# A scan followed by a mixture of adapters: a second output bank, transposes over a free bank, a split residual matmul and other groups

## The chip, the cores and the metric

One core of a Trainium2 chip. The metric is the time of one execution in microseconds (us), taken on the device; shorter is better. The profile gives, for one execution, the span from the first to the last instruction; in the runs here the time is about 1.8 us above the span of the same run (213.81 against 212.0 us).

Engine names as in the profile: PE is TensorE (matmuls), PEld its weight loads, DVE is VectorE, ACT is ScalarE, POOL is GpSimd, SP is SyncE, which issues the loads and stores.

## The reference

```python
def _attn_ref(a, b):                 # a, b: (8, 6400, 128) fp32
    for t in range(S):
        h = a[:, t] * h + b[:, t]    # a scan along the sequence
        out[:, t] = h

def _moe_ref(x, w_gate, A, B):       # x: (51200, 128), 8 experts of rank 16, best 2 of 8
    logits = x @ w_gate
    topk = best two of logits;  w = softmax of those two
    delta = sum over the two of  w * (x @ A[e]) @ B[e]
    return x + delta
```

So 52.4 MB are read and 26.2 MB written, and each row goes through the scan, a gating of 8 logits, a product with 8 x 16 gated columns, and the addition of the row itself (the residual).

## The kernel before

The 51200 rows are 100 units of 512. For each unit w the kernel adds operations to a plan with an estimated cost, a priority ("key") and the operations they wait for; the plan then fixes the order of each engine before the launch. The operations of a unit, with the names used below:

- A, B (TensorE): four fp32 transposes each, of a into the bank pA and of b into pB (two banks).
- aev (ACT): copy of pA; scan (VectorE): 512 steps from that copy and pB into xT (fp16).
- L (TensorE): logits into pL. Per group of units, gating: copy of pL (ACT), first maximum (VectorE), three steps on GpSimd, second maximum (VectorE), four steps on GpSimd, sigmoid (ACT).
- Z (TensorE): x times A of all experts into pZ (two banks); mul (VectorE): gated product zw.
- T (TensorE): transposes of zw into pT; tev (ACT): copy of pT.
- R (TensorE): expert matmul and residual matmul into pO; oev (ACT): copy of pO; then the store.

The matmul outputs lie in PSUM, in eight buffers of one bank each: pA, pB, pB, pL, pZ, pZ, pT, pO.

```python
    NZ, NO = 2, 1                               # banks of pZ and of pO
    groups = cut((), 4, (2, 1, 1))              # gating groups: 24 x 4, then 2, 1, 1
    ...
        pL = sb(nc.psum_tensor("pL", [128, 512], F32))
        pT = sb(nc.psum_tensor("pT", [128, 1024], F16))
        pO = [sb(nc.psum_tensor(f"pO{i}", [128, UT], F32)) for i in range(NO)]
    ...
            add(f"Z{w}", "pe", w + 5, 230.0, emit, [f"scan{w}", f"mul{w - NZ}", "cst"])
    ...     # mul{w} waits for Z{w}, the sigmoid of its group, T{w - 2}
            add(f"T{w}", "pe", w + 6, 225.0, emit, [f"mul{w}", f"tev{w - 1}", "idh"])
    ...
        def delta(w):
            def emit(h):
                for i in range(Q):
                    c = o[:, i * 128 : (i + 1) * 128]
                    h.matmul(c, zwT[w % 2][:, i * 128 : (i + 1) * 128], Bcat_h, start=True, stop=False)
                    last = h.matmul(c, x_block(w, i), ident_h[:, :], start=False, stop=True)
                return last
            add(f"R{w}", "pe", w + 6.5, 455.0, emit, [f"tev{w}", f"oev{w - NO}"])
    ...     # oev{w} on ACT waits for R{w}
```

Of the kernel before, what the change touches and what calls it, by code (L numbers as in the profile page):

```python
# [12 lines left out]
PRINT = False  # L13


class _Op:


    def __init__(self, name, eng, key, busy, lat, emit, deps, dma):
        self.name = name  # L20
        self.eng = eng
        self.key = key
        self.busy = busy
        self.lat = lat
        self.emit = emit
        self.deps = deps
        self.dma = dma
        self.signal = False
        self.done = None


class _Plan:
# [7 lines left out]
    def add(self, name, eng, key, busy, lat, emit, deps=(), dma=None):  # L40
        self.ops[name] = _Op(name, eng, key, busy, lat, emit, list(deps), dma)

    def schedule(self, dma_rate):
# [8 lines left out]
        end = {}  # L52
        cand = {e: [] for e in self.sems}
        free = {e: 0.0 for e in self.sems}
        link = 0.0
        for op in ops.values():
            if not left[op.name]:
                cand[op.eng].append((0.0, op))
        todo = len(ops)
        while todo:  # L60
            best = None
            for e, c in cand.items():
                if c:
                    t = max(free[e], min(r for r, _ in c))
                    if best is None or t < best[0]:
                        best = (t, e)
            t, e = best
            pick = min((x for x in cand[e] if x[0] <= t), key=lambda x: (x[1].key, x[0]))
            cand[e].remove(pick)
            op = pick[1]  # L70
            self.order[e].append(op)
            free[e] = t + op.busy
            if op.dma:
                link = max(link, t + op.busy + 1500.0) + op.dma[2] / dma_rate
                end[op.name] = link + op.lat
            else:
                end[op.name] = t + op.busy + op.lat
            todo -= 1
            for u in users[op.name]:
                left[u.name] -= 1  # L80
                if not left[u.name]:
                    cand[u.eng].append((max(end[d.name] for d in u.deps), u))
# [30 lines left out]
def bass_associative_scan_2x2__then__mixture_of_adapters_kernel(  # L113
# [20 lines left out]
    NZ, NO = 2, 1  # L134
    NOUT = 16

# [18 lines left out]
    groups = cut((), 4, (2, 1, 1))  # L155
# [11 lines left out]
    with ExitStack() as stack:  # L167
# [34 lines left out]
        pL = sb(nc.psum_tensor("pL", [128, 512], F32))  # L202
        pZ = [sb(nc.psum_tensor(f"pZ{i}", [128, UT], F32)) for i in range(NZ)]
        pT = sb(nc.psum_tensor("pT", [128, 1024], F16))
# [8 lines left out]
        def add(name, eng, key, busy, emit, deps=(), dma=None):  # L213
            lat = {"pe": 190.0, "dve": 120.0, "act": 150.0, "pool": 100.0, "sp": 100.0}[eng]
            plan.add(name, eng, key, busy, lat, emit, deps, dma)
# [115 lines left out]
        def logits(w):  # L331
# [9 lines left out]
            add(f"L{w}", "pe", w + 1, 140.0, emit, [f"scan{w}", f"lev{k - 1}", "cst"])  # L341

        def gating(k):
# [3 lines left out]
            key = u0 + n + 0.5  # L347
            fixed = 60.0 + 75.0 * (4 - n)
# [4 lines left out]
            def bc(t):  # L353
# [8 lines left out]
                [f"L{w}" for w in range(u0, u0 + n)] + [f"p4_{k - 2}", f"p3_{k - 2}", f"p6_{k - 2}"],  # L362
            )
# [10 lines left out]
                "pool",  # L374
                key,
                410.0,
# [5 lines left out]
                "pool",  # L382
                key,
                650.0,
# [5 lines left out]
                "pool",  # L390
                key,
                460.0,
# [13 lines left out]
                "pool",  # L406
                key,
                410.0,
# [5 lines left out]
                "pool",  # L414
                key,
                650.0,
# [5 lines left out]
                "pool",  # L422
                key,
                460.0,
# [5 lines left out]
                "pool",  # L430
                key,
                460.0,
# [13 lines left out]
        def z_mm(w):  # L446
# [5 lines left out]
            add(f"Z{w}", "pe", w + 5, 230.0, emit, [f"scan{w}", f"mul{w - NZ}", "cst"])  # L452

        def z_mul(w):
# [3 lines left out]
            zview = pZ[w % NZ][:, :].rearrange("p (q e r) -> p q e r", q=Q, e=E, r=R)  # L458
            oview = zw[w % 2][:, :, :].rearrange("p q (e r) -> p q e r", e=E)
            add(  # L460
                f"mul{w}",
                "dve",
                w + 5.5,
                600.0,
                lambda h: h.tensor_tensor(out=oview, in0=zview, in1=gview, op=ALU.mult),  # L465
                [f"Z{w}", f"sig{k}", f"T{w - 2}"],
            )

        def zw_tr(w):
            def emit(h):  # L470
                for i in range(Q):
                    last = h.transpose(pT[:, i * 128 : (i + 1) * 128], zw[w % 2][:, i, :], ident_h[:, :])  # L472
                return last

            add(f"T{w}", "pe", w + 6, 225.0, emit, [f"mul{w}", f"tev{w - 1}", "idh"])

        def t_evac(w):
# [5 lines left out]
                lambda h: h.copy(zwT[w % 2][:, :], pT[:, 0:UT]),  # L483
                [f"T{w}", f"R{w - 2}"],
            )

        def delta(w):
            o = pO[w % NO]

            def emit(h):  # L490
                for i in range(Q):
                    c = o[:, i * 128 : (i + 1) * 128]
                    h.matmul(c, zwT[w % 2][:, i * 128 : (i + 1) * 128], Bcat_h, start=True, stop=False)  # L493
                    last = h.matmul(c, x_block(w, i), ident_h[:, :], start=False, stop=True)  # L494
                return last

            add(f"R{w}", "pe", w + 6.5, 455.0, emit, [f"tev{w}", f"oev{w - NO}"])

        def o_evac(w):
            add(  # L500
                f"oev{w}",
                "act",
                w + 6.5,
                480.0,
                lambda h: h.copy(outt[:, w % NOUT, :], pO[w % NO][:, :]),  # L505
                [f"R{w}", f"st{store_of.get(w - NOUT)}"],
# [39 lines left out]
        print("plan", plan.span) if PRINT else None  # L546
# [49 lines left out]
```

## Time and profile before

The median was 221.71 us (three executions). The profiled execution has a span of 221.2 us.

The table of windows gives, for a stretch, the busy time of PE, PEld, DVE, ACT and POOL (with instructions), then the granted TensorE clock, the DMA share and GB/s. The kernel before, steady stretch and drain (from the last scan to the end):

```profile
40.00:190.00 150.00, 150.00 (x2156) 148.85 (x2155) 145.57 (x197) 131.96 (x270) 66.85 (x134) 1.00 1.05 398
197.35:221.20 23.85, 12.55 (x169) 10.21 (x166) 7.98 (x16) 13.14 (x29) 7.89 (x25) 0.84 0.39 145
```

In the steady stretch TensorE counts as busy all the time, its weight loads 99%, VectorE 97%, and DMA moves 398 GB/s. In the 23.85 us of the drain no engine is busy for more than about 55% (ACT, 13.14 us).

VectorE in that drain (timeline of the kernel before: start, duration, instruction, count, and in brackets the idle time before it and what ended it):

```profile
197.35 1.27 DVE L313 TENSOR_TENSOR_SCAN xT<-a_st,xT,pB 128x512 f16<-128x512 f32 x1
198.54 0.67 DVE L465 TENSOR_TENSOR zw<-pZ,g 128x512 f16<-128x512 f32 x1
...
202.77 0.69 DVE L465 TENSOR_TENSOR zw<-pZ,g 128x512 f16<-128x512 f32 x1 [0.51 <-PE pT L472]
...
204.63 0.69 DVE L465 TENSOR_TENSOR zw<-pZ,g 128x512 f16<-128x512 f32 x1 [0.71 <-PE pT L472]
206.51 0.69 DVE L465 TENSOR_TENSOR zw<-pZ,g 128x512 f16<-128x512 f32 x1 [1.18 <-PE pT L472]
```

The products come one every 1.87 us, each held up by the transposes. The transposes stand on TensorE behind R, which waits for both copies on ACT. ACT in the same stretch:

```profile
206.28 0.59 ACT L505 COPY outt<-pO 128x512 f32<-128x512 f32 x1 [0.64 <-PE pO L494]
206.77 0.59 ACT L483 COPY zwT<-pT 128x512 f16<-128x512 f16 x1
207.24 0.24 ACT L442 ACTIVATE g<-um 128x32 f32<-128x32 f32 x1
208.15 0.59 ACT L505 COPY outt<-pO 128x512 f32<-128x512 f32 x1 [0.67 <-PE pO L494]
```

This is a ring over single buffers: copy of pO, R, T, product, Z, one after the other.

### The profile page before, as it was taken

The numbers are of one execution on the slowest core, as the hardware profiler recorded it, in microseconds if no ns is written. First come the engines' busy times: TensorE is split into PE (matmuls) and PEld (weight loads), VectorE is DVE, ScalarE is ACT, GpSimd is POOL, SyncE is SP. The second block draws the span as 40 slices with busy tenths as digits, with TensorE's granted clock in tenths as the row PEclk, the third lists the DMA queues.
The fourth block names the chain that finished last, engine by engine and source line by source line (L and its number), as shares of the span: only waits on it lengthen the run. The fifth ranks groups of instructions, "written<-read, shape, count | busy, mean of one in ns | idle before, by whom it ended". The sixth has DMA issues, their size and how long they took to land.

```text
span 221.2 us, 6969 instructions
## 1 busy us (share of the span) xinstructions
PE 204.4 (92%) x2800; PEld 195.6 (88%) x2800; DVE 191.5 (87%) x261; ACT 174.2 (79%) x356; POOL 90.5 (41%) x195
## 2 busy tenths in 40 slices
PE   3889999999999999999999999999999999987552
PEld 2767889999999999999999999999999999985441
DVE  0499999999999999999999999999999999994320
ACT  3245589888889888888888898888899888876653
POOL 1016425435353543534445253443535435357400
PEclk9999999999999999999999999999999999999985
DMA  7999999999999999999999999999999999843434
GB/s 183 379 387 387 385 385 388 385 402 402 398 402 398 398 400 399 399 399 397 399 397 398 402 398 402 397 397 402 398 398 401 395 400 400 320 180 134 156 131 153
DMA packets 42208, 79.23 MB, mean 358 GB/s; under 512 B 3648, under 2 KB 3776, under 8 KB 42176
## 3 DMA queue, kind: packets, MB, share of 16 engines
q1 hardware_dynamic: 40848, 78.65, 94.3%
q8 instruction: 22, 0.36, 0.7%
q10 hardware_dynamic: 1328, 0.14, 0.5%
q14 instruction: 10, 0.08, 0.1%
HBM read 52.56 MB, written 26.21 MB: 356 GB/s over the span
## 4 chain that ended last, share of the span: by engine, by line
PE 82%; DVE 7%; ACT 3%; DMA 2%; issue 2%; POOL 1%; SPq 1%; DVEq 0%; ACTq 0%; POOLq 0%
PE pA L282 19%; PE pB L282 18%; PE pZ L449 12%; PE pO L493 10%; PE pO L494 10%; PE pT L472 9%; DVE xT L313 5%; PE pL L338 5%; DMA b_in<-in_b_dram 2%; DVE zw L465 2%; ACT outt L505 2%; ACT zwT L483 1%; SPq L266 1%; POOL pn L417 0%; ACT a_st L296 0%
## 5 line engine op out<-in xcount | busy, mean ns | idle before, releaser
L313 DVE TENSOR_TENSOR_SCAN xT<-a_st,xT,pB 128x512 f16<-128x512 f32 x96 | 120.0, 1250 | 3.4 <-PE pB L282 1.6
L505 ACT COPY outt<-pO 128x512 f32<-128x512 f32 x100 | 58.9, 589 | 28.3 <-PE pO L494 27.5
L465 DVE TENSOR_TENSOR zw<-pZ,g 128x512 f16<-128x512 f32 x100 | 67.3, 674 | 10.9 <-PE pT L472 5.8
L296 ACT COPY a_st<-pA 128x512 f32<-128x512 f32 x100 | 59.3, 593 | 12.8 <-PE pA L282 8.3
L282 PE MATMUL pA<-ident_f,a_in 128*128 128x128 f32 x400 | 63.1, 281 | 3.8 <-DMA a_in<-in_a_dram 3.8
L282 PE MATMUL pB<-ident_f,b_in 128*128 128x128 f32 x400 | 61.2, 277 | 0.1
L493 PE MATMUL pO<-cst_h,zwT 128*128 128x128 f16 x400 | 56.2, 221 | 4.8 <-ACT zwT L483 4.8
L483 ACT COPY zwT<-pT 128x512 f16<-128x512 f16 x100 | 58.9, 589 | 0.4 <-PE pT L472 0.4
L494 PE MATMUL pO<-ident_h,xT 128*128 128x128 f16 x400 | 56.2, 221 | 0.0
L282 PEld LDWEIGHTS pA<-ident_f,a_in 128*128 128x128 f32 x400 | 43.0, 143 | 5.3 <-DMA a_in<-in_a_dram 4.2
L282 PEld LDWEIGHTS pB<-ident_f,b_in 128*128 128x128 f32 x400 | 46.9, 142 | 0.9 <-DMA b_in<-in_b_dram 0.9
L494 PEld LDWEIGHTS pO<-ident_h,xT 128*128 128x128 f16 x400 | 45.1, 114 | 1.0
L493 PEld LDWEIGHTS pO<-cst_h,zwT 128*128 128x128 f16 x400 | 39.2, 99 | 6.3 <-ACT zwT L483 6.1
L449 PE MATMUL pZ<-cst_h,xT 128*128 128x128 f16 x400 | 40.7, 225 | 3.6 <-DVE zw L465 3.5
L472 PE MATMUL pT<-ident_h,zw 128*128 128x128 f16 x400 | 39.0, 220 | 0.0
L449 PEld LDWEIGHTS pZ<-cst_h,xT 128*128 128x128 f16 x400 | 26.4, 117 | 5.0 <-DVE zw L465 4.5
L338 PE MATMUL pL<-cst_h,xT 128*128 128x8 f16 x400 | 27.4, 174 | 1.3 <-DVE xT L313 0.9
L472 PEld LDWEIGHTS pT<-ident_h,zw 128*128 128x128 f16 x400 | 26.7, 98 | 0.0
L338 PEld LDWEIGHTS pL<-cst_h,xT 128*128 128x128 f16 x400 | 23.5, 117 | 3.6 <-DVE xT L313 3.4
L377 POOL TENSOR_TENSOR d_0<-Lg,m_0 128x128 f32<-128x128 f32 (+2 forms) x14 | 5.4, 388 | 36.2 <-DVE m_0 L369 36.2
L409 POOL TENSOR_TENSOR d_0<-Lg,m_0 128x128 f32<-128x128 f32 (+2 forms) x14 | 5.5, 390 | 25.7 <-DVE m_0 L401 25.7
L409 POOL TENSOR_TENSOR d_1<-Lg,m_1 128x128 f32<-128x128 f32 (+1 forms) x13 | 5.2, 397 | 23.7 <-DVE m_1 L401 23.2
(29 smaller groups left out, 114.5 us busy)
## 6 DMA issues: line engine op xcount, KB each, us to landing
a_in<-in_a_dram SPq DMA_DIRECT2D x49, 512.0 KB, 11.2
b_in<-in_b_dram SPq DMA_DIRECT2D x49, 512.0 KB, 11.3
out_dram<-outt SPq DMA_DIRECT2D x49, 512.0 KB, 11.1
a_in<-in_a_dram SPq DMA_DIRECT2D x2, 256.0 KB, 3.6
b_in<-in_b_dram SPq DMA_DIRECT2D x2, 256.0 KB, 4.3
out_dram<-outt SPq DMA_DIRECT2D x2, 256.0 KB, 2.0
cst_f<-in_moe_A_dram ACTq DMA_DIRECT2D x1, 64.0 KB, 4.0
cst_f<-in_moe_B_dram ACTq DMA_DIRECT2D x1, 64.0 KB, 4.4
```

Source lines behind the costliest of these rows:

```text
L282: last = h.transpose(view[:, i, :], ring[:, w % RING, i * 128 : (i + 1) * 128], ident_f[:, :])
L296: lambda h: h.copy(a_st[w % 2][:, :], pA[:, :]),
L313: last = h.tensor_tensor_scan(out=xT[:, x0 + lo : x0 + hi], data0=a_st[w % 2][:, lo:hi], data1=pB[w % 2][:, lo:hi], initial=init, op0=ALU. ...
L338: last = h.matmul(pL[:, c : c + E], x_block(w, i), wg_h)
L409: lambda h: h.tensor_tensor(out=v(d2[s]), in0=v(Lg[s]), in1=bc(m2[s]), op=ALU.subtract),
L449: last = h.matmul(pZ[w % NZ][:, i * 128 : (i + 1) * 128], x_block(w, i), Acat_h)
L465: lambda h: h.tensor_tensor(out=oview, in0=zview, in1=gview, op=ALU.mult),
L472: last = h.transpose(pT[:, i * 128 : (i + 1) * 128], zw[w % 2][:, i, :], ident_h[:, :])
L483: lambda h: h.copy(zwT[w % 2][:, :], pT[:, 0:UT]),
L493: h.matmul(c, zwT[w % 2][:, i * 128 : (i + 1) * 128], Bcat_h, start=True, stop=False)
L494: last = h.matmul(c, x_block(w, i), ident_h[:, :], start=False, stop=True)
L505: lambda h: h.copy(outt[:, w % NOUT, :], pO[w % NO][:, :]),
```

## The change

The intent is a shorter drain and an earlier start of the products:

1. R is split: the residual matmul (R) no longer waits for the copy of zw, only the expert matmul (D) does. The flag start is set on the first of the four blocks only (start=i==0).
2. pO gets two banks. To make room, pL and pT share one bank (pTL); the plan gets "banks", and keeps two engines from being in one at a time.
3. In the last 10 units every second transposition goes into pA, which is free then, and every second output copy goes to VectorE.
4. The last group is one of four units, gated on VectorE with priority; the first groups are 1, 1, 2.
5. Other priorities (Z, T, R, D).

```diff
-    NZ, NO = 2, 1
+    NZ, NO = 2, 2
+    TAIL = 10
+    KZ, KT, KR, KD = 8, 8.2, 8.6, 8.0
-    groups = cut((), 4, (2, 1, 1))
+    groups = cut((1, 1, 2), 4, ())
-        pL = sb(nc.psum_tensor("pL", [128, 512], F32))
-        pT = sb(nc.psum_tensor("pT", [128, 1024], F16))
+        pTL = sb(nc.psum_tensor("pTL", [128, 512], F32))
+        pT = pTL[:, 0 : UT // 2].bitcast(F16)
+        pL = pTL[:, UT // 2 : UT // 2 + GB * E]
 ...  (gating)
-            key = u0 + n + 0.5
+            key = u0 + n + (0.5 if k < len(groups) - 1 else -6)
+            ge = "dve" if k == len(groups) - 1 else "pool"      # seven steps, were "pool"
 ...  (transposes of zw, their copy)
+        def spare(w):
+            return w >= NU - TAIL and w % 2 == 1
+        def t_dst(w):
+            return pA[:, 0 : UT // 2].bitcast(F16) if spare(w) else pT
-            add(f"T{w}", "pe", w + 6, 225.0, emit, [f"mul{w}", f"tev{w - 1}", "idh"])
+            add(f"T{w}", "pe", w + KT, 225.0, emit,
+                [f"mul{w}", "idh", f"tev{w - 2 if w > NU - TAIL else w - 1}"] + [f"aev{NU - 1}"] * spare(w),
+                bank=t_bank(w))
 ...  (residual and expert matmul)
-            add(f"R{w}", "pe", w + 6.5, 455.0, emit, [f"tev{w}", f"oev{w - NO}"])
+            add(f"R{w}", "pe", w + KR, 226.0, emit_x, [f"scan{w}", f"oev{w - NO}", "idh"])
+            add(f"D{w}", "pe", w + KD, 226.0, emit_d, [f"R{w}", f"tev{w}", "cst"])
 ...  (output copy)
+            oe = "dve" if w >= NU - TAIL and w % 2 == 0 else "act"
```

In the plan's scheduler (not shown) an operation with a bank starts only when the last operations of the other engines on that bank have ended, and then waits for them.

More of the change, by code (lines that the diff above doesn't have):

```diff
@@ L10, with __init__ @@
 AX = mybir.AxisListType
-PRINT = False
 class _Op:
-    def __init__(self, name, eng, key, busy, lat, emit, deps, dma):
+    def __init__(self, name, eng, key, busy, lat, emit, deps, dma, bank):
         self.name = name
@@ L27, in __init__ @@
         self.dma = dma
+        self.bank = bank
         self.signal = False
@@ L38, in __init__, with add @@
         self.order = {e: [] for e in sems}
-    def add(self, name, eng, key, busy, lat, emit, deps=(), dma=None):
-        self.ops[name] = _Op(name, eng, key, busy, lat, emit, list(deps), dma)
+    def add(self, name, eng, key, busy, lat, emit, deps=(), dma=None, bank=None):
+        self.ops[name] = _Op(name, eng, key, busy, lat, emit, list(deps), dma, bank)
     def schedule(self, dma_rate):
@@ L55, in schedule @@
         link = 0.0
+        bank = {}
         for op in ops.values():
@@ L62, in schedule @@
             for e, c in cand.items():
-                if c:
-                    t = max(free[e], min(r for r, _ in c))
-                    if best is None or t < best[0]:
-                        best = (t, e)
-            t, e = best
-            pick = min((x for x in cand[e] if x[0] <= t), key=lambda x: (x[1].key, x[0]))
+                for x in c:
+                    other = [end[o.name] for o in bank.get(x[1].bank, {}).values() if o.eng != e]
+                    t = max([free[e], x[0]] + other)
+                    if best is None or (t, x[1].key) < best[:2]:
+                        best = (t, x[1].key, e, x)
+            t, _, e, pick = best
             cand[e].remove(pick)
             op = pick[1]
+            if op.bank:
+                held = bank.setdefault(op.bank, {})
+                op.deps += [o for o in held.values() if o.eng != e]
+                held[e] = op
             self.order[e].append(op)
@@ L211, in bass_associative_scan_2x2__then__mixture_of_adapters_kernel, with add @@
         plan = _Plan(sems)
-        def add(name, eng, key, busy, emit, deps=(), dma=None):
+        def add(name, eng, key, busy, emit, deps=(), dma=None, bank=None):
             lat = {"pe": 190.0, "dve": 120.0, "act": 150.0, "pool": 100.0, "sp": 100.0}[eng]
-            plan.add(name, eng, key, busy, lat, emit, deps, dma)
+            plan.add(name, eng, key, busy, lat, emit, deps, dma, bank)
         def add_dma(name, eng, key, emit, slot, nbytes, deps=()):
@@ L339, in emit @@
                 return last
-            add(f"L{w}", "pe", w + 1, 140.0, emit, [f"scan{w}", f"lev{k - 1}", "cst"])
+            add(f"L{w}", "pe", w + 1, 140.0, emit, [f"scan{w}", f"lev{k - 1}", "cst"], bank="TL")
         def gating(k):
@@ L346, in gating, with cost @@
             s = k % 2
-            key = u0 + n + 0.5
-            fixed = 60.0 + 75.0 * (4 - n)
+            key = u0 + n + (0.5 if k < len(groups) - 1 else -6)
+            ge = "dve" if k == len(groups) - 1 else "pool"
+            def cost(t):
+                return 200.0 if ge == "dve" else t
             def v(t):
@@ L362, in gating @@
                 [f"L{w}" for w in range(u0, u0 + n)] + [f"p4_{k - 2}", f"p3_{k - 2}", f"p6_{k - 2}"],
+                bank="TL",
             )
@@ L373, in gating @@
                 f"p1_{k}",
-                "pool",
+                ge,
                 key,
-                410.0,
+                cost(410.0),
                 lambda h: h.tensor_tensor(out=v(d1[s]), in0=v(Lg[s]), in1=bc(m1[s]), op=ALU.subtract),
@@ L381, in gating @@
                 f"p2_{k}",
-                "pool",
+                ge,
                 key,
-                650.0,
+                cost(650.0),
                 lambda h: h.tensor_scalar(v(pn[s]), v(d1[s]), 0.0, -1.0e30, ALU.is_ge, ALU.mult),
@@ L389, in gating @@
                 f"p3_{k}",
-                "pool",
+                ge,
                 key,
-                460.0,
+                cost(460.0),
                 lambda h: h.tensor_tensor(out=v(L2[s]), in0=v(Lg[s]), in1=v(pn[s]), op=ALU.add),
@@ L405, in gating @@
                 f"p4_{k}",
-                "pool",
+                ge,
                 key,
-                410.0,
+                cost(410.0),
                 lambda h: h.tensor_tensor(out=v(d2[s]), in0=v(Lg[s]), in1=bc(m2[s]), op=ALU.subtract),
@@ L413, in gating @@
                 f"p5_{k}",
-                "pool",
+                ge,
                 key,
-                650.0,
+                cost(650.0),
                 lambda h: h.tensor_scalar(v(pn[s]), v(d2[s]), 0.0, -1.0e30, ALU.is_lt, ALU.mult),
@@ L421, in gating @@
                 f"p6_{k}",
-                "pool",
+                ge,
                 key,
-                460.0,
+                cost(460.0),
                 lambda h: h.tensor_tensor(out=v(d1[s]), in0=v(d1[s]), in1=v(d2[s]), op=ALU.add),
@@ L429, in gating @@
                 f"p7_{k}",
-                "pool",
+                ge,
                 key,
-                460.0,
+                cost(460.0),
                 lambda h: h.tensor_tensor(out=v(um[s]), in0=v(d1[s]), in1=v(pn[s]), op=ALU.add),
@@ L450, in emit @@
                 return last
-            add(f"Z{w}", "pe", w + 5, 230.0, emit, [f"scan{w}", f"mul{w - NZ}", "cst"])
+            add(f"Z{w}", "pe", w + KZ, 230.0, emit, [f"scan{w}", f"mul{w - NZ}", "cst"])
         def z_mul(w):
@@ L457, in z_mul, with t_bank @@
             gview = g[k % 3][:, o : o + Q, :].unsqueeze(3).broadcast_to([128, Q, E, R])
-            zview = pZ[w % NZ][:, :].rearrange("p (q e r) -> p q e r", q=Q, e=E, r=R)
             oview = zw[w % 2][:, :, :].rearrange("p q (e r) -> p q e r", e=E)
+            deps = [f"sig{k}", f"T{w - 2}"]
+            src = pZ[w % NZ]
+            eng, busy, deps = "dve", 600.0, deps + [f"Z{w}"]
+            zview = src[:, :].rearrange("p (q e r) -> p q e r", q=Q, e=E, r=R)
             add(
                 f"mul{w}",
-                "dve",
+                eng,
                 w + 5.5,
-                600.0,
+                busy,
                 lambda h: h.tensor_tensor(out=oview, in0=zview, in1=gview, op=ALU.mult),
-                [f"Z{w}", f"sig{k}", f"T{w - 2}"],
+                deps,
             )
+        def spare(w):
+            return w >= NU - TAIL and w % 2 == 1
+        def t_dst(w):
+            return pA[:, 0 : UT // 2].bitcast(F16) if spare(w) else pT
+        def t_bank(w):
+            return "A" if spare(w) else "TL"
         def zw_tr(w):
@@ L471, in emit @@
                 for i in range(Q):
-                    last = h.transpose(pT[:, i * 128 : (i + 1) * 128], zw[w % 2][:, i, :], ident_h[:, :])
+                    last = h.transpose(t_dst(w)[:, i * 128 : (i + 1) * 128], zw[w % 2][:, i, :], ident_h[:, :])
                 return last
-            add(f"T{w}", "pe", w + 6, 225.0, emit, [f"mul{w}", f"tev{w - 1}", "idh"])
+            add(
+                f"T{w}",
+                "pe",
+                w + KT,
+                225.0,
+                emit,
+                [f"mul{w}", "idh", f"tev{w - 2 if w > NU - TAIL else w - 1}"] + [f"aev{NU - 1}"] * spare(w),
+                bank=t_bank(w),
+            )
         def t_evac(w):
@@ L482, in t_evac, with emit_x, emit_d @@
                 480.0,
-                lambda h: h.copy(zwT[w % 2][:, :], pT[:, 0:UT]),
-                [f"T{w}", f"R{w - 2}"],
+                lambda h: h.copy(zwT[w % 2][:, :], t_dst(w)),
+                [f"T{w}", f"D{w - 2}"],
+                bank=t_bank(w),
             )
         def delta(w):
-            o = pO[w % NO]
-            def emit(h):
+            def emit_x(h):
                 for i in range(Q):
-                    c = o[:, i * 128 : (i + 1) * 128]
-                    h.matmul(c, zwT[w % 2][:, i * 128 : (i + 1) * 128], Bcat_h, start=True, stop=False)
-                    last = h.matmul(c, x_block(w, i), ident_h[:, :], start=False, stop=True)
-                return last
-            add(f"R{w}", "pe", w + 6.5, 455.0, emit, [f"tev{w}", f"oev{w - NO}"])
+                    last = h.matmul(
+                        pO[w % NO][:, i * 128 : (i + 1) * 128],
+                        x_block(w, i),
+                        ident_h[:, :],
+                        start=i == 0,
+                        stop=False,
+                        skip_group_check=True,
+                    )
+                return last
+            def emit_d(h):
+                for i in range(Q):
+                    last = h.matmul(
+                        pO[w % NO][:, i * 128 : (i + 1) * 128],
+                        zwT[w % 2][:, i * 128 : (i + 1) * 128],
+                        Bcat_h,
+                        start=False,
+                        stop=True,
+                        skip_group_check=True,
+                    )
+                return last
+            add(f"R{w}", "pe", w + KR, 226.0, emit_x, [f"scan{w}", f"oev{w - NO}", "idh"])
+            add(f"D{w}", "pe", w + KD, 226.0, emit_d, [f"R{w}", f"tev{w}", "cst"])
         def o_evac(w):
+            oe = "dve" if w >= NU - TAIL and w % 2 == 0 else "act"
             add(
                 f"oev{w}",
-                "act",
+                oe,
                 w + 6.5,
-                480.0,
-                lambda h: h.copy(outt[:, w % NOUT, :], pO[w % NO][:, :]),
-                [f"R{w}", f"st{store_of.get(w - NOUT)}"],
+                600.0 if oe == "dve" else 480.0,
+                lambda h: (h.tensor_copy if oe == "dve" else h.copy)(outt[:, w % NOUT, :], pO[w % NO][:, :]),
+                [f"D{w}", f"st{store_of.get(w - NOUT)}"],
             )
@@ L545, in bass_associative_scan_2x2__then__mixture_of_adapters_kernel @@
         plan.schedule(390.0)
-        print("plan", plan.span) if PRINT else None
         block = sb(nc.Block())
```

## The prediction

> **What bounds the kernel now.** Three stages.
> 1. Ramp to about 24 us: VectorE scans from 6.3 us (timeline).
> 2. Steady state, 24 to 197 us: the table of windows shows matmul and weight loads both at 99-100% from 40 to 190 us, VectorE at 97%, DMA at 398 GB/s. The timeline shows TensorE without a gap: a unit of 512 rows takes 7.80 us / 4 = 1.95 us (A transposes start at 185.89 and 193.69). The chain of waits is 82% TensorE. The Trainium skill (Perfetto Trace Analysis, head note) calls matmul busy time a bad measure and weight-load busy a good one; here both agree, and the 55 ns pitch of the fp16 matmuls confirms it.
> 3. Drain: the last scan starts at 197.35 us, and 23.9 us follow. Nothing is saturated: TensorE 6.8 of 10.7 us, ACT 7.1, VectorE 5.9. Nine gated products (zw) remain and start 1.87 us apart, in a ring of latencies that the chain shows: zw 0.70 -> Z matmul 0.41 -> residual+expert matmul 0.65, in program order -> transpose 0.24 -> zw. There is one pO bank and one transpose bank. The last gatings (2, 1, 1 units) add GpSimd steps of 0.24-0.65 us.
>
> **What the change does.** Matmul, transpose and copy counts stay. Residual matmuls no longer wait for the zw copy, only the expert half does. pO gets a second bank by merging logits and transposes into one; the plan then keeps engines apart on that bank (the skill, PSUM — Partial Sum Buffer, Terms, calls two engines in one bank an error; no run here shows that). For the last 10 units, transposes alternate with the free pA bank and half of the output copies go to VectorE. The last group is four units, gated on VectorE: seven operations which I estimate at 0.2 us each, from the 0.28 us reduction and the 0.67 us product (512 elements), against 0.41-0.65 us on GpSimd.
>
> **Steady state: no gain.** Same TensorE work, already back to back. The order listing shows the same lag: when scan 16 or scan 96 is issued, 8 and 88 products have gone (before: 8 and 87). One unit more is done before the last scan: +0.7 us. I walked a cycle of four units: no chain exceeds 7.8 us. Loads: the last one issues at 178 us, lands about 190 us, is used at 193.7 us; one store now goes ahead earlier, about 1.3 us; slack remains.
>
> **Ramp:** two residual blocks go in earlier, small groups add reductions: 0 to +0.4 us.
>
> **Drain:** I walked the new order with traced durations. From the start of the last scan: gating done and sigmoid at 8.2 us, interleaved with four products; last four products end at 11.3; last expert matmul 13.3; last copy 14.0; store 2.6 (as before: 218.6 to 221.2). That is 16.6 us, plus 0.3 us for the lower clock that this sparse stage got before (0.53). 17 us instead of 23.9.
>
> Sum: last scan at 198.2, end at 215.2 us of span; timed runs are 0.5 us above it: **215.5 us** (-2.8%), range 212.5 to 219. Chances: faster 0.76, same 0.21, slower 0.03.
>
> **Signs.** Right: 40-190 us still 100% matmul and near 399 GB/s; last scan at 197.5-199; zw spacing in the drain below 1.3 us apart from one gap of under 2 us at the last gating; drain about 17 us. Wrong: TensorE gaps behind the merged bank (logits or transposes waiting for ACT), or transposes of a waiting for DMA at the end.
>
> **What would make it wrong.** The fixed order stalling TensorE in the steady state (1% is 2 us); VectorE gating slower than 0.2 us a step; the clock dropping earlier; or a ramp that saves more than I see.

## More of the kernel before

Timeline of the kernel before, a product on VectorE:

```profile
186.88 0.67 DVE L465 TENSOR_TENSOR zw<-pZ,g 128x512 f16<-128x512 f32 x1
```

and TensorE around its end, from T to the next A:

```profile
187.22 0.39 PE L472 MATMUL pT<-ident_h,zw 128*128 128x128 f16 x4
187.44 0.27 PE L338 MATMUL pL<-cst_h,xT 128*128 128x8 f16 x4
187.60 0.41 PE L449 MATMUL pZ<-cst_h,xT 128*128 128x128 f16 x4
187.85 0.61 PE L282 MATMUL pA<-ident_f,a_in 128*128 128x128 f32 x4
```

Busy times of matmuls overlap (0.27 us from 187.44 runs past 187.60), so only the distances of the starts tell the pace. L to Z is 0.16 us here. Z starts 0.05 us after the product ends, at 187.55.

## The result

The changed kernel took 214.12 us (median of four, 213.81 to 214.45) against 222.56 us before: ratio 0.962, 95% interval 0.956 to 0.968. Ratios here are the mean time of one kernel's runs over that of the other's in the same rounds, so not quite the ratio of the medians. The output was correct in all executions, before and after, and in all experiments.

Windows of the changed kernel, steady stretch and drain from the last scan:

```profile
40.00:190.00 150.00, 149.89 (x2180) 148.50 (x2179) 147.21 (x198) 128.41 (x273) 68.19 (x137) 1.00 1.05 398
195.59:212.00 16.41, 10.90 (x146) 8.36 (x144) 11.33 (x24) 9.21 (x19) 1.56 (x3) 1.00 0.55 204
```

The drain went from 23.85 to 16.41 us, and VectorE is busy 69% of it instead of 33%. The last scan comes 1.76 us earlier too. VectorE in the drain of the changed kernel:

```profile
195.59 1.27 DVE L319 TENSOR_TENSOR_SCAN xT<-a_st,xT,pB 128x512 f16<-128x512 f32 x1
196.98 0.69 DVE L553 COPY outt<-pO 128x512 f32<-128x512 f32 x1
197.59 0.27 DVE L379 TENSOR_REDUCE m_0<-Lg 128x16 f32<-128x128 f32 x1
...
198.58 0.68 DVE L478 TENSOR_TENSOR zw<-pZ,g 128x512 f16<-128x512 f32 x1
199.18 0.22 DVE L395 TENSOR_SCALAR pn<-d_0 128x128 f32<-128x128 f32 x1
199.31 0.68 DVE L478 TENSOR_TENSOR zw<-pZ,g 128x512 f16<-128x512 f32 x1
...
202.92 0.29 DVE L443 TENSOR_TENSOR um<-d_0,pn 128x128 f32<-128x128 f32 x1
203.59 2.70 DVE L478 TENSOR_TENSOR zw<-pZ,g 128x512 f16<-128x512 f32 x4 [0.37 <-ACT g L452]
```

No product waits for a transposition any more. The gating steps stand between the products, and the last four products wait for the gating alone.

ACT in the changed drain, the copies of the last transposes and outputs:

```profile
206.18 0.58 ACT L513 COPY zwT<-pTL 128x512 f16<-128x512 f16 x1 [0.22 <-PE pTL L494]
206.66 0.59 ACT L553 COPY outt<-pO 128x512 f32<-128x512 f32 x1
207.14 0.60 ACT L513 COPY zwT<-pA 128x512 f16<-128x512 f16 x1
208.31 0.58 ACT L553 COPY outt<-pO 128x512 f32<-128x512 f32 x1 [0.56 <-PE pO L533]
```

And the steady stretch of the changed kernel. The same transition of TensorE as above:

```profile
160.84 0.39 PE L494 MATMUL pTL<-ident_h,zw 128*128 128x128 f16 x4
161.06 0.27 PE L344 MATMUL pTL<-cst_h,xT 128*128 128x8 f16 x4
161.19 0.39 PE L459 MATMUL pZ<-cst_h,xT 128*128 128x128 f16 x4
161.42 0.61 PE L288 MATMUL pA<-ident_f,a_in 128*128 128x128 f32 x4
```

L to Z is 0.13 us now, not 0.16, and Z to A is 0.23, not 0.25 (the means between 60 and 180 us are 0.129 against 0.158, and 0.228 against 0.250). So these two held pauses of TensorE, not work. VectorE in a later cycle of the same kernel:

```profile
187.88 2.69 DVE L319 TENSOR_TENSOR_SCAN xT<-a_st,xT,pB 128x512 f16<-128x512 f32 x2
190.49 1.26 DVE L478 TENSOR_TENSOR zw<-pZ,g 128x512 f16<-128x512 f32 x2
191.67 0.27 DVE L379 TENSOR_REDUCE m_1<-Lg 128x16 f32<-128x128 f32 x1
191.86 1.27 DVE L319 TENSOR_TENSOR_SCAN xT<-a_st,xT,pB 128x512 f16<-128x512 f32 x1
193.05 0.66 DVE L478 TENSOR_TENSOR zw<-pZ,g 128x512 f16<-128x512 f32 x1
193.63 1.27 DVE L319 TENSOR_TENSOR_SCAN xT<-a_st,xT,pB 128x512 f16<-128x512 f32 x1
194.82 0.26 DVE L411 TENSOR_REDUCE m_1<-L_1 128x16 f32<-128x128 f32 x1
195.00 0.68 DVE L478 TENSOR_TENSOR zw<-pZ,g 128x512 f16<-128x512 f32 x1
```

Two scans stand next to each other here, and then two products (x2 counts them). From the first scan's start to the first product's it is 2.61 us; from a scan's start to that of a product behind it, it is 1.19 us (191.86 to 193.05). The experiments come back to this.

### Where the 9.2 us of span went

I took the starts of the copies of pA from the timelines of both kernels. The copy of unit 4 starts at 12.63 us before and 12.32 us after, but over all runs below anywhere from 12.0 to 14.1 us, for a reason that has nothing to do with the change (last section). So I count from there; "pace" is the distance of the copies of units 28 and 92, divided by 64.

| stretch, us | before | after | gain |
|---|---|---|---|
| start to copy of unit 4 | 12.63 | 12.32 | 0.3 (jitter) |
| unit 4 to 28 | 45.05 | 43.97 | 1.1 |
| unit 28 to 92 (pace 1.952, 1.926) | 124.94 | 123.29 | 1.65 |
| unit 92 to 99 | 13.68 | 13.64 | 0.0 |
| copy of unit 99 to last scan | 1.05 | 2.37 | -1.3 |
| last scan to end (drain) | 23.85 | 16.41 | 7.4 |

The drain is the main gain. But 1.65 us came from a pace that I had called fixed, and 1.1 us from units 4 to 28 (12 to 57 us; at unit 10, about 22 us, the changed kernel is still 1.1 us behind, at unit 20 it leads by 0.3), and 1.3 us went back before the last scan, where the changed order has one product more and stands with its last scan behind it.

### The profile page after: what moved, and what is told of

The parts are those of the page before. It is cut to its first block, busy times and chain, and to the rows that moved or that the text cites. A ratio compares the mean times of both kernels' runs of the same rounds, so it can differ in the third digit from the quotient of the medians.

```text
span 212.0 us, 7066 instructions
## 1 busy us (share of the span) xinstructions
PE 201.3 (95%) x2800; PEld 192.9 (91%) x2800; DVE 195.6 (92%) x273; ACT 166.7 (79%) x351; POOL 86.9 (41%) x188
## 4 chain that ended last, share of the span: by engine, by line
PE 77%; DVE 16%; issue 2%; DMA 2%; ACT 1%; SPq 0%; DVEq 0%
PE pB L288 18%; PE pA L288 18%; DVE xT L319 11%; PE pO L521 9%; PE pO L533 9%; PE pZ L459 9%; PE pTL L494 8%; PE pTL L344 5%; DVE zw L478 3%; DMA a_in<-in_a_dram 2%; DVE outt L553 1%; ACT outt L553 1%; SPq L272 0%; PE pA L494 0%; DVE m_0 L379 0%
## 5 line engine op out<-in xcount | busy, mean ns | idle before, releaser
L513 ACT COPY zwT<-pTL 128x512 f16<-128x512 f16 x95 | 56.9, 598 | 2.9 <-PE pTL L494 2.7
L288 PEld LDWEIGHTS pB<-ident_f,b_in 128*128 128x128 f32 x400 | 43.0, 143 | 1.0 <-DMA b_in<-in_b_dram 0.4
L521 PE MATMUL pO<-ident_h,xT 128*128 128x128 f16 x400 | 38.9, 220 | 1.5 <-ACT outt L553 0.7
L533 PE MATMUL pO<-cst_h,zwT 128*128 128x128 f16 x400 | 38.6, 219 | 0.3
L494 PE MATMUL pTL<-ident_h,zw 128*128 128x128 f16 x380 | 36.8, 220 | 0.0
L521 PEld LDWEIGHTS pO<-ident_h,xT 128*128 128x128 f16 x400 | 31.5, 114 | 3.1 <-DVE outt L553 1.3
L533 PEld LDWEIGHTS pO<-cst_h,zwT 128*128 128x128 f16 x400 | 27.5, 97 | 2.1 <-PE pO L521 0.7
L344 PE MATMUL pTL<-cst_h,xT 128*128 128x8 f16 x400 | 27.3, 174 | 1.2 <-DVE xT L319 1.0
L344 PEld LDWEIGHTS pTL<-cst_h,xT 128*128 128x128 f16 x400 | 23.6, 116 | 3.2 <-DVE xT L319 2.7
L494 PEld LDWEIGHTS pTL<-ident_h,zw 128*128 128x128 f16 x380 | 25.0, 98 | 0.1
```

Of the source, the lines that this page charges most:

```text
L288: last = h.transpose(view[:, i, :], ring[:, w % RING, i * 128 : (i + 1) * 128], ident_f[:, :])
L344: last = h.matmul(pL[:, c : c + E], x_block(w, i), wg_h)
L494: last = h.transpose(t_dst(w)[:, i * 128 : (i + 1) * 128], zw[w % 2][:, i, :], ident_h[:, :])
L513: lambda h: h.copy(zwT[w % 2][:, :], t_dst(w)),
L521: last = h.matmul(pO[w % NO][:, i * 128 : (i + 1) * 128], x_block(w, i), ident_h[:, :], start=i == 0, stop=False, skip_group_check=True,)
L533: last = h.matmul(pO[w % NO][:, i * 128 : (i + 1) * 128], zwT[w % 2][:, i * 128 : (i + 1) * 128], Bcat_h, start=False, stop=True, skip_gro ...
```

## The experiments

Twelve kernels. As the plan orders all engines anew when an operation changes, a "single part" below means that part and the order that follows from it, unless I say that the order was the same. "Aligned end" is the span minus the start of the copy of unit 4, from one profile each; the last column is its difference to the changed kernel's. The changed kernel stands for comparison at 214.12 us. The intervals of the ratios are +-0.5 to 0.7%, so differences of under 2 us between kernels are not settled by them alone. For these I use the aligned end, which agrees within 0.15 us where only something without effect was changed (before and b_ring, changed and a_noself), and the traces.

| run | what | median us | ratio to before (95%) | pace | drain | aligned end | to the changed kernel |
|---|---|---|---|---|---|---|---|
| before | | 222.56 | 1 | 1.952 | 23.85 | 208.57 | +8.89 |
| changed | | 214.12 | 0.962 (0.956-0.968) | 1.926 | 16.41 | 199.68 | 0 |
| b_ring | before, a GpSimd step cut | 222.39 | 1.002 (0.996-1.007) | 1.952 | 23.76 | 208.43 | +8.75 |
| b_groups | before, first groups 1, 1, 2 | 221.90 | 1.001 (0.994-1.007) | 1.942 | 25.57 | 208.70 | +9.02 |
| b_dve | before, maxima cut | 221.06 | 0.993 (0.986-0.999) | 1.936 | 23.61 | 206.44 | +6.76 |
| a_tail0 | no rotation | 218.54 | 0.982 (0.977-0.986) | 1.927 | 19.89 | 203.17 | +3.49 |
| a_poolgate | last gating on GpSimd | 213.40 | 0.960 (0.955-0.966) | 1.926 | 15.65 | 198.93 | -0.75 |
| a_fused | no split | 212.85 | 0.956 (0.950-0.962) | 1.910 | 18.54 | 198.59 | -1.09 |
| a_onebank | one output bank | 220.92 | 0.992 (0.986-0.998) | 1.963 | 21.77 | 207.11 | +7.43 |
| a_groups4 | first groups of four | 212.83 | 0.955 (0.948-0.962) | 1.918 | 17.70 | 198.23 | -1.45 |
| a_noself | no wait of TensorE for itself | 214.18 | 0.961 (0.954-0.968) | 1.926 | 16.30 | 199.57 | -0.11 |
| a_last211 | last groups 2, 1, 1 | 216.16 | 0.972 (0.965-0.979) | 1.927 | 18.16 | 201.57 | +1.89 |
| s_best | candidate | 211.98 | 0.952 (0.945-0.959) | 1.918 | 17.05 | 197.62 | -2.06 |
| f_warm | candidate | 212.51 | 0.954 (0.948-0.960) | 1.910 | 18.02 | 198.07 | -1.61 |

Drains compare only where the order up to the last scan is the same (changed, a_tail0, a_poolgate, a_noself); else a longer drain can mean that the last scan came earlier, with more products left. The aligned end has no such catch.

### What carries the drain

**a_onebank**: one output bank again.

```diff
-    NZ, NO = 2, 2
+    NZ, NO = 2, 1
```

> The changed kernel with one output bank, split kept. Theory BANKS: residual of the next unit cannot start before the copy of the last one, so TensorE waits and the drain is 2 to 5 us longer; the steady pace may rise above 1.927. Rival SPLIT: under 1 us.

Measured: 220.92 us. Nearly the whole gain is gone: the drain is 21.77 us (5.4 more) and the pace 1.963 (0.036 a unit more, 2.3 us over units 28 to 92). BANKS holds; the drain's loss is just above its range. TensorE in that kernel's drain:

```profile
211.23 0.41 PE L521 MATMUL pO<-ident_h,xT 128*128 128x128 f16 x4 [0.56 <-DVE outt L553]
211.70 0.40 PE L533 MATMUL pO<-cst_h,zwT 128*128 128x128 f16 x4
212.77 0.61 PE L521 MATMUL pO<-ident_h,xT 128*128 128x128 f16 x4 [0.68 <-ACT outt L553]
```

Each residual waits for the copy of the unit before, although the copies go to two engines in turn. The split and the rotation are of little use without the bank.

**a_tail0**: TAIL = 0, so neither the spare transposition bank nor output copies on VectorE. The order is the same as in the changed kernel up to the last units.

> The changed kernel without the rotation in the last 10 units: one transpose bank, all output copies on ACT. Same order until the last scan. Theory TAIL: ACT then does both copies of each unit and transposes wait for the single bank, about 1.1 us a unit instead of 0.65, so the drain from the last scan grows from 16.4 to 18 to 19.5 us and the total by 1.5 to 3 us. Rival: split and second output bank alone shorten the drain; then under 0.7 us.

Measured: 218.54 us, 4.4 us longer by the medians, 3.5 us by the aligned end; the drain is 19.89 us. TAIL holds, with a loss above its range (1.5 to 3 us). The run takes away the spare bank and the copies on VectorE together, so their shares stay open. The products wait for the single transposition bank again, 1.64 us apart:

```profile
207.20 0.69 DVE L478 TENSOR_TENSOR zw<-pZ,g 128x512 f16<-128x512 f32 x1 [0.96 <-PE pTL L494]
208.84 0.69 DVE L478 TENSOR_TENSOR zw<-pZ,g 128x512 f16<-128x512 f32 x1 [0.94 <-PE pTL L494]
```

**a_last211**: `groups = cut((1, 1, 2), 4, (2, 1, 1))`.

> The changed kernel with last groups of 2, 1, 1 as before (the last single unit gated on VectorE). Theory LAST: three more gatings put 2 x 7 GpSimd steps of 0.24 to 0.44 us and three sigmoids in the drain, so it is 1 to 3 us longer than with one group of four. Rival: the last unit's gating is on 32 columns instead of 128 and ends sooner, the products before it hide it; within 0.7 us of the changed kernel.

Measured: 216.16 us, 2.0 us longer (1.9 aligned). LAST holds: on VectorE the last product starts at 208.52 us, behind three gatings in a row, where the changed kernel ends its last at 206.29.

**a_poolgate**: the last gating on GpSimd like all others; same order until the last gating.

```diff
-            ge = "dve" if k == len(groups) - 1 else "pool"
+            ge = "pool"
```

> The changed kernel with the last gating on GpSimd as all others. Theory INTENT (as the change and my prediction have it): VectorE gating is faster, so the last four products start later than 8.0 us after the last scan's start, and the total grows by 1 to 2 us. Rival INTERLEAVE: on VectorE the seven steps stand between products and output copies and take 5.6 us from first maximum to last sum, on GpSimd about 4.6 us with VectorE free; then the last products start 0.3 to 1 us earlier, and the total is 0 to 1 us shorter.

Measured: 213.40 us. The drain is 15.65 us, 0.76 us less than with VectorE. INTERLEAVE holds: the last products start 7.24 us after the last scan's start (203.39 against 196.15), before 8.00 (203.59 against 195.59).

```profile
202.78 0.69 DVE L553 COPY outt<-pO 128x512 f32<-128x512 f32 x1 [0.97 <-PE pO L533]
203.39 2.69 DVE L478 TENSOR_TENSOR zw<-pZ,g 128x512 f16<-128x512 f32 x4
```

A step takes 0.22 to 0.29 us on VectorE against 0.41 to 0.65 on GpSimd. But on VectorE it stands in one line with products and output copies: from first maximum to last sum 5.6 us (197.59 to 203.21), on GpSimd 4.8 us (198.15 to 202.92), with VectorE free for the products. The part of the change that looked cheapest costs 0.75 us.

**a_fused**: residual and expert matmul in one operation again, as before; two banks, rotation, groups as changed.

```diff
 ...  (one emit with both matmuls per block, as before, in place of two)
-            add(f"R{w}", "pe", w + KR, 226.0, emit_x, [f"scan{w}", f"oev{w - NO}", "idh"])
-            add(f"D{w}", "pe", w + KD, 226.0, emit_d, [f"R{w}", f"tev{w}", "cst"])
+            add(f"D{w}", "pe", w + KD, 452.0, emit, [f"tev{w}", f"oev{w - NO}", "cst"])
```

> The changed kernel with residual and expert matmuls together again as before (both wait for the zw copy), two output banks, merged bank, rotation and groups kept. Theory BANKS: the second bank and the rotation carry the drain, the split does little, since the four residual matmuls take only 0.22 us: the total changes by less than 0.8 us. Rival SPLIT: getting the residual out of the chain is what shortens the drain; then it is at least 1.5 us longer.

Measured: 212.85 us, 1.3 us shorter than with the split (1.1 aligned). SPLIT falls. BANKS was right in that the split does not help, but I had not expected it to cost something. Its pace is 1.910, the fastest of all. The next experiments say why.

### What sets the pace

**b_ring**: the kernel before, with one GpSimd step of 0.46 us cut to one element (the output was still within the reference's tolerance); order unchanged.

> The kernel before, order of all engines kept, but the sixth gating step on GpSimd (the sum of the two differences, 0.46 us) reduced to one element. Results are wrong on purpose. Theory RING: before, the steady pace of 1.952 us a unit is set by a ring second maximum -> four GpSimd steps -> sigmoid -> product, in which VectorE waits 0.23 us in every four units for the sigmoid; taking 0.46 us out removes that wait and the pace falls to 1.925 to 1.935, so that the last a copy starts 1.5 to 2.5 us earlier and the total is about 2 us (0.9%) shorter. Rival PITCH: the pace is TensorE's own, from the order of its groups (transposes right behind logits take 0.47 instead of 0.44 us); then the pace stays at 1.950 +- 0.003 although the sigmoid wait is gone, and the total changes by less than 0.5 us.

Measured: nothing moved, 222.39 us, pace 1.952. The sigmoid wait of 0.23 us stayed as well, so the experiment did not do what it was meant to, and it can't decide between its theories. A look at ACT in the kernel before shows why:

```profile
191.31 0.59 ACT L505 COPY outt<-pO 128x512 f32<-128x512 f32 x1 [0.30 <-PE pO L494]
191.80 0.59 ACT L483 COPY zwT<-pT 128x512 f16<-128x512 f16 x1
192.27 0.32 ACT L442 ACTIVATE g<-um 128x128 f32<-128x128 f32 x1
```

The last GpSimd step had ended at 191.81 (191.35 plus 0.46), and the sigmoid starts at 192.27, when its turn on ACT comes. An earlier GpSimd does not help it. That gave RING2: TensorE up to R, then two copies and the sigmoid on ACT, product, maximum, scan and product on VectorE, then Z on TensorE.

**b_dve**: the kernel before, same order, both maxima over one block instead of 16 (0.07 us each instead of 0.19; the numbers of the gating are wrong on purpose, and stayed within the tolerance).

```diff
-                lambda h: h.tensor_reduce(out=m1[s][:, 0:c], in_=v(Lg[s]), axis=AX.X, op=ALU.max),
+                lambda h: h.tensor_reduce(out=m1[s][:, 0:1], in_=Lg[s][:, 0:1, :], axis=AX.X, op=ALU.max),
```

(and likewise m2; both cleared once at the start)

> The kernel before, order of all engines kept, with both maximum reductions cut to one block (0.19 us of VectorE each becomes about 0.07), wrong on purpose. The first ring test did not loosen the sigmoid wait, because the sigmoid stands on ACT behind the copy of pO and the copy of pT, not behind GpSimd. Theory RING2: the pace before, 1.952 us a unit, is closed by a ring through three engines: Z matmul waits for a product, TensorE 3.7 us, two copies and sigmoid on ACT, product, first maximum, scan, product, Z matmul. TensorE's own groups need only 1.926. Shortening the maximum by 0.13 us then brings the pace to 1.925 to 1.938, Z behind logits from 0.25 to 0.23 us, and the last a copy (taken from the copy of unit 24 on) comes 1.0 to 2.0 us earlier. Rival PITCH: VectorE is not in it, TensorE's order of groups costs that much; the pace stays at 1.950 +- 0.003.

Measured: pace 1.9355, within RING2's range and far from PITCH's; the last a copy comes 1.15 us earlier, counted from unit 24. On TensorE the mean distance of Z to the next A behind logits fell from 0.249 to 0.238 us, and in half of the cases the pause is gone:

```profile
185.64 0.27 PE L343 MATMUL pL<-cst_h,xT 128*128 128x8 f16 x4
185.77 0.39 PE L454 MATMUL pZ<-cst_h,xT 128*128 128x128 f16 x4
186.00 0.61 PE L287 MATMUL pA<-ident_f,a_in 128*128 128x128 f32 x4
```

So the kernel before was not TensorE at its own pace: a saving of 0.12 us on VectorE, twice in four units, moved a TensorE that counted as 100% busy. VectorE alone did not set the pace either, since its wait for the sigmoid grew from 0.23 to 0.37 us. That the ring runs through ACT is read from the timeline (the sigmoid behind two copies, and these behind R); no run shortened ACT.

**a_noself**: the changed kernel, same order, but D does not wait on TensorE's own semaphore (the counter by which an operation learns that another has ended) for R before it on the same engine (the waits for other engines stay).

```diff
             for d in op.deps:
+                if d.eng == eng == "pe":
+                    continue
                 sem, value = d.done
```

> The changed kernel, same order, but the expert matmul no longer waits on TensorE's own semaphore for the residual matmul before it on the same engine. Theory SELF: this wait drains the pipeline where the two follow each other (0.27 instead of 0.22 us, once in four units), the pace falls from 1.926 to 1.915 +- 0.003 us a unit and the total by 0.5 to 1.2 us. Rival: the 0.05 us are the wait for the copy of zw on ACT; no change of pace.

Measured: the pause went, R to D is 0.22 us now where it was 0.27 (mean of 15 and 14 cases between 60 and 180 us), but the pace stayed at 1.926, and the time at 214.18 us. So the wait was TensorE's for itself, as SELF says, and yet it cost nothing: in the same stretch A behind R starts after 0.249 us instead of 0.225, and R behind B after 0.455 instead of 0.443, so the pause came back elsewhere. TensorE, 99% busy in its weight loads, does not set the pace of the changed kernel. VectorE does: the lines of the changed kernel above show two scans in a row taking 2.61 us from 187.88 to the product at 190.49. The scan before a product takes 1.19 us, so the first of the two takes about 1.41. Its order repeats every four units (from 187.88 to 195.59, 7.71 us; the list of waits between 40 and 190 us has none of VectorE, and the trace has no idle time of it there but some 0.13 us between two scans in a row, 2.8 us in all): two scans, two products, maximum, scan, product, scan, maximum, product. That is 1.93 us a unit, the measured pace. In the order scan, product, scan, product no scan follows a scan. The second scan of a pair starts 0.13 us after the end of the first (187.88 plus 1.28 and 0.13, so at 189.29). It needs the last element of the first, and by the plan it also waits on VectorE's own semaphore for it, as D did on TensorE's. Where a unit of two sequences is scanned in two halves inside one operation, without such a wait and without that need, the second half (256 columns) starts 0.65 us after the first, before the first has ended (it counts as 0.74 us). No run separates the wait from the need; a_noself took away the waits of TensorE only.

With that, a_fused falls into place: its VectorE order is scan, product, scan, product almost throughout, and its TensorE order has no L in front of fp32 transposes except once in four or more units. Adding the distances of its groups (0.443 + 0.436 + 0.447 + 0.223 + 0.129 + 0.228 for A, B, R with D, T, L, Z) gives 1.906 us, next to its pace of 1.910. By itself such a sum is close to the pace in any kernel whose TensorE has no other groups; what counts is that no distance holds a pause: L to Z (0.129) and Z to A (0.228) are as short as in the changed kernel, where TensorE had time to spare. So this kernel seems to run at TensorE's own pace, with VectorE, which waits 1.2 us in 150, close behind; no experiment on it tests that.

### The start

**b_groups**: the kernel before with `groups = cut((1, 1, 2), 4, (2, 1, 1))`.

> The kernel before with first groups of 1, 1 and 2 units, last groups of 2, 1, 1 kept. Theory GROUPS: the 1.3 us that the changed kernel leads by at unit 20 come from the small first groups (products start at 16.4 instead of 22.3 us), so this kernel leads the kernel before by 1.0 to 1.6 us at unit 20 and is about 1.3 us shorter if its new order keeps the steady pace. Rival SPLIT: the lead comes from residual matmuls that fill TensorE early; then the lead at unit 20 is under 0.4 us.

Measured, counted from unit 4: a lead of 0.5 us at unit 20, 1.5 at unit 24, and an aligned end 0.1 us later than before. (Counted so, the changed kernel leads by 0.3 us at unit 20 and by 1.0 at unit 24; the 1.3 us of the expectation was too much.) A lead of the scans is no gain by itself: the drain grew from 23.85 to 25.57 us, the products that had not been made came later. Neither theory saw that; the small groups alone save nothing.

**a_groups4**: the changed kernel with `groups = cut((), 4, ())`.

> The changed kernel with first groups of four (25 groups of 4, last one still four units). Theory GROUPS: counted from the copy of unit 4 (to leave the slow first transposes out, which differ from run to run by up to 1.4 us), the small first groups gave 0.8 to 1.1 us at unit 24; without them this kernel is that much behind at unit 24 and 0.5 to 1.3 us longer. Rival: the lead is given back, because the lag of products behind scans is the same from unit 16 on; total within 0.5 us or even shorter.

Measured: 212.83 us, 1.3 us shorter (1.45 aligned), so the rival holds and more. Without the small groups, VectorE's order has scans and products in turn, and the pace is 1.918. That is 0.5 of the 1.45 us, over units 28 to 92; another 0.5 lies between units 4 and 28 (43.45 against 43.97) and 0.4 behind unit 92. The small first groups had shifted the order of the whole run, and cost time all along it.

### Candidates

**s_best**: the changed kernel with groups of four, gating on GpSimd, no wait of TensorE for itself, and seven matmuls on the identity from 1.5 us.

```diff
+        def warm_up(h):
+            for i in range(7):
+                last = h.matmul(pZ[0][:, 0:128], ident_f[:, :], ident_f[:, :])
+            return last
+        add("warm_up", "pe", -9, 2000.0, warm_up, ["id"])
 ...  (and the edits of a_groups4, a_poolgate and a_noself)
```

> Candidate: the changed kernel with groups of four throughout, last gating on GpSimd, no wait of TensorE for itself, and seven idle matmuls on the identity at 1.5 us so that the slow first transposes (1.1 us for four instead of 0.6) are paid while TensorE waits for the first load. If the single effects add: 1.3 + 0.7 + 0.8 + 1 us off 214.1, so 210.3 us, 209 to 212. Rival: loads bind (they land at about 188 us in the changed kernel and b of unit 98 is transposed at 191); then transposes of the last units show waits for DMA and the total stays above 212.

Measured: 211.98 us, the lowest median (the single times of f_warm, median 212.51, overlap with its own): 1% under the changed kernel, ratio 0.952 to before. No transposition waits for DMA in the last 30 us, so the rival falls, but the sum was 210.3: the self-wait was worth nothing, and so was the start.

**f_warm**: a_fused with the same seven matmuls.

> Candidate: the kernel with residual and expert matmul together (212.85 us) with the seven idle matmuls at the start. Theory CLOCK: the copy of unit 4, which starts at 12.1 to 14.1 us in all runs so far, starts below 12 us, and the total is 0.5 to 2 us shorter than 212.85. Rival: idle matmuls end in time but TensorE is as slow after them; then the copy of unit 4 is not earlier.

Measured: 212.51 us, 0.3 us under a_fused. The copy of unit 4 starts at 12.03 (12.48 in s_best), not below 12. The clock part is right, the gain is not: behind the idle matmuls the first four transposes take 0.60 us instead of 1.12, but they start at 4.65 instead of 3.5 to 3.8 us, and then the first scan starts at 6.29 us, as without. On VectorE it stands behind the cast of the constants, whose load lands at about 6 us.

```profile
6.07 0.30 DVE L261 CAST cst_h<-cst_f 128x264 f16<-128x264 f32 x1 [4.34 <-DMA cst_f<-in_moe_B_dram]
6.29 1.21 DVE L326 TENSOR_TENSOR_SCAN xT<-a_st,pB 128x512 f16<-128x512 f32 x1
```

Not run, and so open: the fused matmul together with groups of four and the gating on GpSimd; the first scan ahead of the cast; the old priorities (part 5 of the change); one output bank without the split; the changed kernel without VectorE's waits for itself. The second output bank was run with the merged bank only; in the changed kernel's steady stretch the list of waits has no wait of TensorE for a copy on it.

## Why the prediction was right or wrong

The time was right: 215.5 us predicted, 214.12 measured, in the range, and faster by over 2% with a chance of 0.76. Its parts were less so.

- **The drain: right.** "17 us instead of 23.9": 16.41. The last copy came 13.3 us after the last scan's start (predicted 14.0), the store took 3.1 (2.6), and the clock did not fall (0.3 us set aside). a_onebank, a_tail0 and a_last211 show that bank, rotation and the single last group carry it. The sign "one gap of under 2 us" was off: the gap is 2.6 us.
- **"Steady state: no gain. Same TensorE work, already back to back": wrong**, 1.65 us over units 28 to 92. The step that failed was to read 100% matmul and 99% weight-load busy as TensorE without a pause. The Trainium skill (Perfetto Trace Analysis, Identifying the Most-Contended Engine) names MFU (the matmul work done as a share of the peak), which I did not work out, and weight-load busy as the measures for TensorE; in this trace the latter reads 99% before, while pauses of 0.02 to 0.03 us at Z were hidden in it, and 99% after, while VectorE set the pace. The distance of the starts shows what the busy time hides. "I walked a cycle of four units: no chain exceeds 7.8 us" was about the new order only; the ring that held the old one, 7.81 us around, I did not look for. b_dve shows that VectorE is in it.
- **"Ramp: 0 to +0.4 us": missed.** By the end of what I called the ramp (about 22 us, unit 10) the changed kernel's copies are 1.1 us later, counted from unit 4; at unit 28 they are 1.1 us earlier. But 1.3 us are given back before the last scan, and b_groups shows that such a lead need not be a gain.
- **"Last scan at 198.2"**: 195.59, the sum of both points and of a product more, which did not cost the 0.7 us I had added.
- **"Timed runs are 0.5 us above" the span: wrong.** I compared the median of three executions with the span of another one, which had run 1.2 us longer. The offset is 1.8 us. With it, my span of 215.2 (measured 212.0) would have given 217.0 us. So two errors, 3.2 us in the span and 1.3 in the offset, partly cancelled.
- **Gating on VectorE "at 0.2 us each"**: the steps were 0.22 to 0.29 us, and the sigmoid was done 8.0 us after the last scan's start (predicted 8.2). But I compared it with the engine's speed and not with the line it would stand in; a_poolgate shows it costs 0.75 us. That the split would be a part of the gain I took from the change's intent; a_fused shows the opposite.
- **The merged bank**: the feared waits did not come. I named the skill's rule of one engine per bank (PSUM — Partial Sum Buffer, Terms); the plan kept to it in all runs, so no run shows what breaking it does.

## What to carry to other kernels

Where several engines are each 90 to 100% busy, look at the distances of the starts, and cut a little from one engine without changing the order: what moves tells who sets the pace. In this drain latency counted and not speed: give each buffer of the ring a second one, spread the copies over two engines, and leave work off the engine that the rest of the drain needs, even if another engine is twice as slow. Undo each part of a bundled change by itself: here the bank, the rotation and the single last group carried the gain (7.4, 3.5 and 1.9 us when one of them is taken away; they overlap, since the whole gain is 8.9), and three other parts (the split, the last gating on VectorE, the small first groups) cost about 0.75 to 1.45 us each.

## What the Trainium skill lacked or had wrong

- Perfetto Trace Analysis, Identifying the Most-Contended Engine: MFU and weight-load busy as the measures for TensorE. Here weight-load busy is 99% in both kernels (148.85 and 148.50 of 150 us), and in neither TensorE alone set the pace (b_dve: 0.12 us off each maximum on VectorE took 0.017 us a unit off; a_noself: a pause less on TensorE changed nothing).
- TensorE: Matmul & The Clock Gate, Part 4, says that the full clock "doesn't engage" for transposes. Here the first fp32 transposes run at half pace (1.12 us for four) and go over to 0.61 to 0.69 us: 3.4 to 4.8 us after the first one in the changed kernel (between 6.83 and 8.24 us, when TensorE had run 16 transposes and 12 fp16 matmuls), 7.8 to 9.5 us after it in b_ring (between 11.55 and 13.26 us). The start jitter goes with it: the copy of unit 4 starts at 12.1 to 12.6 us where the half pace ends by 8.5 us, and at 14.1 us in the two runs where it lasts beyond 12 (b_ring, b_groups). Part 1 of the page gives about 4 us of sustained matmuls, with 0.5 us from run to run; the seven idle matmuls (1.5 to 4.7 us) did make the first transposes fast, the spread without them was larger. The profile's granted clock reads 1.00 all that time.
- VectorE: DVE Perf Modes, The DRAIN you can't avoid, says that a semaphore after each instruction costs nothing extra, for copies. Here a scan of 512 columns takes about 1.41 us instead of 1.19 when the next scan, which needs its last element and waits on VectorE's semaphore for it, follows at once. The page's figure is for copies; for scans no page has one, and whether the wait or the need costs the time stays open.
